# Attention and experts on one core: row scaling put behind the expert choices, row numbers as a sum of tensors, own rooms' gathers asked for sooner, gathered rows turned in three steps

## The chip, the cores and the metric

The kernel runs on one core of a Trainium2 chip. A core has TensorE (PE, matrix products), VectorE (DVE), ScalarE (ACT), GpSimd (POOL) and SyncE (SP), which starts plain transfers; POOL starts the indirect ones (gathers and scatters). The metric is the device time of one execution in microseconds. Each time comes from a median of runs, and one more execution was profiled.

## The reference

```python
# attention: 8 batches, 8 heads, 576 tokens, 64 per head, window of 128, a slope per head
scores = scale * q @ k.T - slope[h] * |rel|      # only 0 <= rel < 128
attn = softmax(scores);  x = (attn @ v) as rows of 512
# experts: per batch, a token takes its own best expert or that of the token before it
fresh_e = argmax(x[b, s] @ w_gate)
e = fresh_e if s == 0 or local_gate[b, s] < 0.5 else prev_e
out[b, s] = softmax(logits[b, s])[e] * (relu(x[b, s] @ w1[e]) @ w2[e])
```

## The kernel before, in words

**Attention.** 35 slots in a row work on 32 pairs of heads, four pairs for a batch. What each engine issues in a slot stands in a table of atoms (`ORDER`): scores `S`, minima `D`, exponentials `E`, transposes `U`, copies `C`, products `M`, results `X`, and `T`, in which DVE transposes the pair's result into the batch's tile `T`. The engines `pe`, `dve`, `act`, `pool` are wrapped in `InOrder`, so each runs its instructions in the order in which the program writes them. Between the atoms, "." advances `side`, the work of the batch that has just ended, and ":", ";" and "," advance three more generators, `gathers`, `early` and `turns`.

**The work of a batch** (`batch_side`) has two halves that advance by turns. `tokens` and `route` compute logits and choices: POOL copies the reciprocals into `rn`, PE makes the logits through the PSUM tile `pk` (its pool has one buffer), DVE forms the products `lw`, then `rm`, `ra`, `rc` and `rcb`, the choice in figures; PE and DVE spread them along the tokens (`hr`), give `OH`, and POOL scatters five times into the table `t4` (`t<-pay,to`). `scaled` is the other half: POOL makes 16 more copies into `rn` and multiplies the four parts of `T` by it (`T<-T,rn`); in the last batch DVE does this on `kr` (`kr<-kr,rn`). `store` then writes `T` to `xd` in DRAM, from which all gathers read.

**Rooms.** The expert part works through rooms, each for one expert. Three own rooms have a fixed expert and size: own0 (256 tokens), own1 (384) and own2 (256); the ranked rooms follow. Own0 and own1 take only tokens of the first batches as far as the tables of batches 5 and 6 know them, and their gathers can run before attention ends. `indices` turns a table into row numbers `xidx` (table entry plus `roff`). A gather (`gather`, POOL, L196) brings 32 rows of a quarter to SBUF; `split_x` turns four of them: DVE transposes into `xtr` (one buffer), ACT casts to `qx`'s high half, DVE subtracts for the low half. Each room has products `h` (with w1) and `y` (with w2), each as three products of halves; `hh` (ACT) and `hl` (DVE) are the halves of `h`, and weights come through `wraw` and are cut into halves `cut` by ACT and DVE.

**What paces the rooms.** `Fixed.run` calls `feed.tick` at points of its program. A tick advances `side` (the routing of batch 7, then the tables of the ranked rooms), turns one tile whose last gather was issued at least `LAG` ticks ago, and issues one gather. `feed.gather` issues none as long as batch 7 is not in `laid`; `ahead` holds gathers that were issued during attention. At a room's end `feed.finish` issues and turns what the next room still lacks.

## Time and profile before

| | |
|---|---|
| median of 3 runs | 691.26 us (690.39 to 691.51) |
| profiled execution | 690.55 us, span 688.8 us |
| mean granted TensorE clock | 0.981 |
| PE busy | 647.2 us, 94% of the span |
| DVE busy | 459.6 us, 67% |
| ACT busy | 413.8 us, 60% |
| POOL busy | 350.2 us, 51% |

The span runs from the first to the last instruction. The granted clock is a share of TensorE's full 2.4 GHz. Attention runs from 0 to about 236 us, own0 from 241.5, own1 from 277, and the ranked rooms from 342. An idle time of an engine stands in brackets in a timeline, with what ended it.

### The profile page before, as it was taken

What the parts mean: (1) busy time and instruction counts of PE and PEld (TensorE: products, weight loads), DVE (VectorE), ACT (ScalarE), POOL (GpSimd) and SP (SyncE); (2) the same over time, 40 slices, a digit from 0 to 9 for tenths busy, and PEclk for the clock granted to TensorE, in tenths of its full rate; (3) what the DMA queues carried; (4) which work ended last, traced back from release to release, by engine and by line L of the source; (5) the groups of instructions that cost most, each with busy time, mean ns of one, the idle gap of its engine ahead of it and who ended that gap; (6) DMA issues with size and microseconds to landing.
All of it is one profiled execution on the core that took longest, in us unless ns stands there. A gap on an engine that the chain in (4) does not pass through costs nothing. (4 is left out here: it accounts for less than half of the span.)

```text
span 688.8 us, 17129 instructions
## 1 busy us (share of the span) xinstructions
PE 647.2 (94%) x5929; PEld 533.8 (77%) x5929; DVE 459.6 (67%) x1434; ACT 413.8 (60%) x1229; POOL 350.2 (51%) x564
## 2 busy tenths in 40 slices
PE   8999999999998579999899999999999999999995
PEld 4777777777675367788689889888888888888884
DVE  7686877778778468776676477475637376655761
ACT  6889898898896553435455465354535354545541
POOL 6365474564737558424777476555735344321011
PEclk9999999999999978999999999999999999999998
DMA  7564765856585067646667577555847566665610
GB/s 233 188 234 138 250 218 153 299 167 211 193 291 168 13 201 234 224 129 209 199 203 242 160 230 239 175 175 173 307 146 273 179 206 224 195 240 167 250 35 31
DMA packets 50314, 134.41 MB, mean 195 GB/s; under 512 B 10967, under 2 KB 13655, under 8 KB 47922
## 3 DMA queue, kind: packets, MB, share of 16 engines
q1 hardware_dynamic: 40706, 113.43, 49.4%
q0 software_dynamic: 9088, 19.29, 9.7%
q8 instruction: 47, 0.77, 0.5%
q10 hardware_dynamic: 432, 0.59, 0.3%
q14 instruction: 41, 0.34, 0.2%
HBM read 113.67 MB, written 19.65 MB: 194 GB/s over the span
## 5 line engine op out<-in xcount | busy, mean ns | idle before, releaser
L196 POOL DMA_INDIRECT kr<-xd,xidx x141 | 160.5, 1138 | 46.1 <-issue 38.3
L291 DVE TENSOR_TENSOR cut<-wraw,cut 128x512 fp32r<-128x512 f32 x215 | 139.5, 685 | 43.2 <-ACT cut L289 41.5
L1008 PE MATMUL h<-qx,cut 128*128 128x256 f32 (+8 forms) x440 | 140.4, 319 | 1.2 <-ACT qx L205 1.2
L1009 PE MATMUL h<-qx,cut 128*128 128x256 f32 (+8 forms) x440 | 139.2, 317 | 0.3 <-DVE qx L206 0.3
L1010 PE MATMUL h<-qx,cut 128*128 128x256 f32 (+8 forms) x440 | 139.5, 317 | 0.0
L289 ACT CAST cut<-wraw 128x512 fp32r<-128x512 f32 x190 | 108.8, 617 | 37.1 <-PE y L1010 37.1
L993 POOL DMA_INDIRECT out<-y,sidx x41 | 45.4, 1107 | 166.2 <-ACT y L1020 133.8
L171 ACT ACTIVATE cut<-scs,mn 128x192 f32<-128x192 f32 (+2 forms) x288 | 123.7, 434 | 8.9 <-DVE mn L171 8.1
L1010 PE MATMUL y<-cut,hl 128*128 128x512 f32 (+2 forms) x288 | 113.0, 396 | 6.3 <-DVE hl L1114 6.2
L1008 PE MATMUL y<-cut,hh 128*128 128x512 f32 (+2 forms) x288 | 114.1, 396 | 2.0 <-ACT hh L171 1.9
L1009 PE MATMUL y<-cut,hh 128*128 128x512 f32 (+2 forms) x288 | 113.9, 395 | 0.0
L1113 ACT ACTIVATE hh<-h 128x256 fp32r<-128x256 f32 (+8 forms) x100 | 45.0, 450 | 114.4 <-PE h L1010 114.0
L1114 DVE SCALAR_TENSOR_TENSOR hl<-h,hh 128x256 fp32r<-128x256 f32 (+8 forms) x112 | 55.5, 495 | 75.8 <-ACT hh L1113 73.5
L171 DVE CUSTOM_DVE_ANT_0 scs<-sc,bias 128x192 f32<-128x192 f32 (+2 forms) x288 | 83.6, 323 | 29.7 <-PE sc L171 19.8
L1008 PEld LDWEIGHTS h<-qx,cut 128*128 128x128 f32 x440 | 84.0, 191 | 15.3 <-issue 9.1
L1009 PEld LDWEIGHTS h<-qx,cut 128*128 128x128 f32 x440 | 84.2, 191 | 4.3 <-DVE qx L206 0.5
L1010 PEld LDWEIGHTS h<-qx,cut 128*128 128x128 f32 x440 | 84.2, 191 | 0.3
L171 PE MATMUL sc<-kr,qx 64*64 64x192 f32 (+2 forms) x1280 | 72.0, 307 | 1.5 <-DVE mn L171 1.5
L1010 PEld LDWEIGHTS y<-cut,hl 128*128 128x128 f32 (+2 forms) x288 | 53.6, 187 | 21.1 <-DVE hl L1114 8.9
L171 PE MATMUL pt<-ident,cut 128*128 128x128 f32 x384 | 62.1, 286 | 0.6 <-DVE mn L171 0.6
L1008 PEld LDWEIGHTS y<-cut,hh 128*128 128x128 f32 (+2 forms) x288 | 54.0, 187 | 11.0 <-ACT hh L171 2.6
L1009 PEld LDWEIGHTS y<-cut,hh 128*128 128x128 f32 (+2 forms) x288 | 53.8, 187 | 9.0 <-issue 0.2
(195 smaller groups left out, 920.3 us busy)
## 6 DMA issues: line engine op xcount, KB each, us to landing
wraw<-w SPq DMA_DIRECT2D x112, 512.0 KB
xT<-w SPq DMA_DIRECT2D x10, 1024.0 KB
kr<-kT SPq DMA_DIRECT2D x31, 288.0 KB
qx<-qT SPq DMA_DIRECT2D x30, 288.0 KB
xd<-T SPq DMA_DIRECT2D x7, 1152.0 KB
v<-v SPq DMA_DIRECT2D x22, 256.0 KB
v<-v SPq DMA_DIRECT2D x32, 128.0 KB
cut<-v SPq DMA_DIRECT2D x10, 256.0 KB
```

What stands on the lines that cost most here:

```text
L171: ins = getattr(self.engine, name)(*args, **kw)
L196: queued(nc.gpsimd.indirect_dma_start(out=r, out_offset=None, in_=src[0:n, :], in_offset=bass.IndirectOffsetOnAxis(ap=col, axis=0), bounds ...
L289: scalar.copy(c[:, 0, f], raw[:, f])
L291: (pool if 2 * n + f == POOL_CUT else vector).tensor_tensor(c[:, 1, f], raw[:, f], c[:, 0, f], ALU.subtract)
L993: ins = nc.gpsimd.indirect_dma_start(out=out[:, :], out_offset=bass.IndirectOffsetOnAxis(ap=col[0:n], axis=0), in_=y[0:n], in_offset=None, ...
L1008: nc.tensor.matmul(o, ah, bh, start=start, stop=False)
L1009: nc.tensor.matmul(o, ah, bl, start=False, stop=False)
L1010: nc.tensor.matmul(o, al, bh, start=False, stop=stop)
L1113: now.act.activation(hh, hp, AF.Relu)
L1114: nc.vector.scalar_tensor_tensor(hl, hp, 0.0, hh, ALU.max, ALU.subtract)
```

## The change

- `scaled`: for all batches but the last, the four scalings of `T` are written only when `route` has appended the batch to `picked` (behind `rcb`), and behind the rooms 4 x `now.calm` further steps. `stores` now gets the batch when the copies are written; the store itself is written when the last scaling is (`scaled_rows`).
- `indices`: `xidx` is a `tensor_tensor` sum with `roff` broadcast instead of a `tensor_scalar` with a value per partition.
- `gathers` is advanced at atom `E5` too, and run to its end behind the last slot; `feed.gather` now holds back as long as batch 7 is in `stores`.
- `split_x` yields between its three steps; `Feed` does one step a tick, `flush` finishes a tile that has been begun. `LAG` is 14 instead of 10.
- `now.held` marks where a tile `pk` is waiting for its reader, and `early` waits while it is set.

```diff
--- before.py
+++ after.py
@@ -182,7 +182,7 @@
         return ins
 
     class Now:
-        calm = 0
+        calm, held = 0, False
 
     now = Now()
 
@@ -202,12 +202,14 @@
         pin(nc.vector.transpose(t, r.rearrange("p q c -> p (q c)")))
         v = t.rearrange("p (q c i) -> p c q i", q=n, c=4)
         xh, xl = (x.rearrange("p c (q i) -> p c q i", q=n) for x in (xh, xl))
+        yield
         now.act.copy(xh, v)
+        yield
         nc.vector.tensor_tensor(xl, v, xh, ALU.subtract)
 
     t4v = t4.rearrange("(t k) w -> t k w", t=32)
 
-    entered, latest, laid, ahead, written = [], [], [], [], []
+    entered, latest, laid, ahead, written, picked, scaled_rows, stores = [], [], [], [], [], [], [], []
 
     def load_table(c0, n, block):
         ins = nc.sync.dma_start(xs[:, c0:c0 + n], t4v[:, block:block + n] if isinstance(block, int) else t4v[:, bass.ds(block, n)])
@@ -223,7 +225,7 @@
 
     def indices(vector, c0, n, w0, wins):
 
-        vector.tensor_scalar(xidx[:, c0:c0 + n], xt[:, c0:c0 + n, 0], roff[:, 0:1], None, ALU.add)
+        vector.tensor_tensor(xidx[:, c0:c0 + n], xt[:, c0:c0 + n, 0], roff.broadcast_to([P, n]), ALU.add)
         yield
         m = len(wins)
         f = tp.tile([P, 48, 2, 4], F32, name="fw", bufs=1)[:, :m]
@@ -264,13 +266,13 @@
                 self.xh, self.xl = self.x[:, 0], self.x[:, 1]
             n = self.last(t)
             sl = slice(P * t, P * t + 32 * n)
-            split_x(self.r[:, t, :n], self.xh[:, :, sl], self.xl[:, :, sl], n)
+            return split_x(self.r[:, t, :n], self.xh[:, :, sl], self.xl[:, :, sl], n)
 
     def at_once(r):
         for t in range(r.n):
             for q in range(4):
                 r.take(t, q)
-            r.turn(t)
+            run(r.turn(t))
 
     def load_chunk(e, which, c):
         src = w1 if which == "a" else w2
@@ -631,16 +633,19 @@
             yield
             for lo, n in ((0, 512), (512, 64)):
                 yield from calm()
+                now.held = True
                 pk = ptk.tile([P, 512], F32, name="pk")
                 for k in range(4):
                     pe.matmul(pk[32 * k:32 * k + 32, :n], w32[:, k], xT[:, k, lo:lo + n], start=True, stop=True)
                 yield
                 act.copy(part[:, lo:lo + n], pk[:, :n])
+                now.held = False
                 yield
             read.append(b)
             by_head = rn[:, 72:112].rearrange("p (h x) -> p x h", h=2)
             for t0, n in ((0, 4), (4, 1)):
                 yield from calm()
+                now.held = True
                 pk = ptk.tile([P, n, 4, 32], F32, name="pk")
                 for t in range(n):
                     pe.transpose(pk[:, t], part[:, P * (t0 + t):P * (t0 + t) + P], ident)
@@ -648,6 +653,7 @@
                 w = tp.tile([P, 16, 2, 9], F32, name="lw", bufs=1)[:, :4 * n]
                 dve.tensor_tensor(w, pk.rearrange("p t k (h f) -> p (t k) h f", h=2)[:, :, :, 0:9],
                                   by_head[:, 4 * t0:4 * t0 + 4 * n].unsqueeze(3).broadcast_to([P, 4 * n, 2, 9]), ALU.mult)
+                now.held = False
                 dve.tensor_reduce(L[:, t0:t0 + n], w.rearrange("p (t k) h e -> p t e (k h)", k=4), AX.X, ALU.add)
                 yield
 
@@ -668,14 +674,17 @@
                             q = 64 * g + 32 * a
                             pool.tensor_copy(rows[q:q + 32, :, o::2, z], rb[c:c + 32, :, o:9:2])
                     yield
+            stores.append(b)
             laid.append(b)
-            while ("T1", 4 * b + 3) not in emitted:
+            while ("T1", 4 * b + 3) not in emitted or b < NB - 1 and b not in picked:
+                yield
+            for _ in range(4 * now.calm):
                 yield
             for p in range(4):
                 t = T[b][:, :, p]
                 (pool if b < NB - 1 else dve).tensor_tensor(t, t, RN[b % 2][:, 18 * p:18 * p + 18].unsqueeze(2).broadcast_to([P, SB, 32]), ALU.mult)
                 if p == 3:
-                    stores.append(b)
+                    scaled_rows.append(b)
                 yield
             if b == NB - 1:
                 store(b)
@@ -704,10 +713,12 @@
             dve.tensor_tensor(a5, a5, k8, ALU.mult)
             dve.tensor_reduce(c, a5, AX.X, ALU.max)
             dve.tensor_tensor(cb, c, fr, ALU.mult)
+            picked.append(b)
             yield
             hr = HR[b % 2]
             for lo, n in ((0, 512), (512, 64)):
                 yield from calm()
+                now.held = True
                 pr = ptk.tile([1, 512], F32, name="pk")
                 w = min(P, n)
                 for t in range(lo // P, (lo + n + P - 1) // P):
@@ -718,8 +729,10 @@
                 yield
                 dve.tensor_tensor_scan(hr[:, lo:lo + n], hold[:, :n], pr[:, :n],
                                        0.0 if lo == 0 else hr[:, lo - 1:lo], ALU.mult, ALU.add)
+                now.held = False
                 yield
             yield from calm()
+            now.held = True
             ph = ptk.tile([P, NT, NE], F32, name="pk")
             for t in range(NT):
                 pe.matmul(ph[:, t], hr[:, P * t:P * t + P], onesb[0:1, 0:NE], start=True, stop=True)
@@ -730,11 +743,13 @@
             yield
             act.activation(ex, ex, AF.Exp)
             dve.tensor_tensor(OH, ph, k8, ALU.is_equal)
+            now.held = False
             yield
 
             assert all(i in bumped for i, n in enumerate(EARLY) if n <= b)
             yield from calm()
             aid = pool if b < NB - 1 else dve
+            now.held = True
             pr = ptk.tile([P, NT, NE], F32, name="pk")
             pe.matmul(pr, utri, OH, start=True, stop=False)
             for t in range(1, NT):
@@ -751,6 +766,7 @@
             rk = tp.tile([P, NT, NE], F32, name="rk")
             ri = tp.tile([P, NT], I32, name="ri")
             dve.tensor_tensor(rk, pr, OH, ALU.mult)
+            now.held = False
             pool.tensor_tensor(pay[:, b, :, 2], gt, se, ALU.mult)
             with nc.allow_low_precision("small whole numbers"):
                 dve.tensor_reduce(ri, rk, AX.X, ALU.add)
@@ -781,6 +797,8 @@
         def early(group):
             while EARLY[group[0]] - 1 not in routed:
                 yield
+            while now.held:
+                yield
             pn = ptk.tile([P, NE], F32, name="pk")
             pe.matmul(pn, onesb, ohs, start=True, stop=True)
             for i in group:
@@ -791,7 +809,9 @@
                 dve.tensor_tensor(ohs[0:1, e:e + 1], ohs[0:1, e:e + 1], d[0:1], ALU.add)
                 bumped.append(i)
                 load_table(col_of[i], OWN_BLOCKS[i], BPE * e)
-            for _ in range(8):
+            for _ in range(5):
+                yield
+            while now.held:
                 yield
             copies(pe, act, col_of[group[0]], sum(OWN_BLOCKS[i] for i in group))
             yield
@@ -828,7 +848,7 @@
                     yield
                 for _ in range(6):
                     yield
-                r.turn(t)
+                yield from r.turn(t)
                 yield
             while not W.raw or NB - 2 not in read:
                 yield
@@ -838,7 +858,7 @@
                     yield
                 yield from W.split(W.room(), act, dve)
 
-        known, bumped, taken, routed, read, emitted, inverted, stores = [], [], [], [], [], [], [], []
+        known, bumped, taken, routed, read, emitted, inverted = [], [], [], [], [], [], []
         rows0 = [Rows(col_of[i], win_of[i], OWN[i][1], n) for i, n in enumerate(EARLY)]
         side, prep = iter(()), {":": setup(), ";": iter(())}
         pairs = {}
@@ -852,7 +872,7 @@
                 else:
                     if i % 11 == 0:
                         yield from ";,"
-                    yield from {"E8": ":", "E3": ":"}.get(atom.strip("'"), "")
+                    yield from {"E8": ":", "E3": ":", "E5": ":"}.get(atom.strip("'"), "")
 
         for slot in range(4 * NB + DEPTH):
             b, p = divmod(slot, 4)
@@ -894,11 +914,11 @@
                     side = batch_side(n // 4, pairs[n][1].xT)
             if 1 <= slot < 4 * NB - 1:
                 values(slot + 1)
-            for n in list(stores):
+            for n in [n for n in stores if n in scaled_rows]:
                 store(n)
             if p == 1 and b + 1 < NB:
                 loaded = load(b + 1)
-        run(chain(prep[";"], prep[","], side))
+        run(chain(prep[";"], prep[":"], prep[","], side))
         last_xT = xT
 
 
@@ -1150,7 +1170,7 @@
         def turn(self, t):
             x = tp.tile([P, 2, 4, P], F32R, name="xT")
             self.xh, self.xl = x[:, 0], x[:, 1]
-            split_x(self.row, self.xh, self.xl)
+            return split_x(self.row, self.xh, self.xl)
 
         def run(self, W, tick):
             y = py.tile([P, DM], F32, name="y")
@@ -1224,10 +1244,10 @@
         table_done.append(1)
 
     class Feed:
-        LAG = 10
+        LAG = 14
 
         def __init__(self, side):
-            self.side, self.clock, self.at, self.turns, self.items = side, 0, 0, [], []
+            self.side, self.clock, self.at, self.turns, self.items, self.step = side, 0, 0, [], [], iter(())
             fixed = [i for i, v in enumerate(visits) if isinstance(v, Fixed)] + [len(visits)]
             for i in [x for a, b in zip(fixed, fixed[1:]) for x in [b] + list(range(a + 1, b)) if x < len(visits)]:
                 r = visits[i].rows
@@ -1245,7 +1265,7 @@
         def gather(self, upto):
             if self.at == len(self.items):
                 return False
-            if NB - 1 not in laid:
+            if NB - 1 in stores or NB - 1 not in laid:
                 return False
             while self.items[self.at] in ahead:
                 ahead.remove(self.items[self.at])
@@ -1266,9 +1286,14 @@
             for x in self.turns:
                 if x[0] <= upto and self.clock >= x[2] + lag:
                     self.turns.remove(x)
-                    visits[x[0]].rows.turn(x[1])
+                    self.step = visits[x[0]].rows.turn(x[1])
+                    next(self.step)
                     return True
             return False
+
+        def flush(self):
+            run(self.step)
+            self.step = iter(())
 
         def tick(self, upto, turn=True):
 
@@ -1276,7 +1301,7 @@
             next(self.side, None)
             if route_done:
                 now.act = nc.scalar
-            if turn:
+            if next(self.step, 0) == 0 and turn:
                 self.turn(upto, self.LAG)
             self.gather(upto)
             if pending and self.clock % 3 == 0:
@@ -1287,9 +1312,11 @@
                 while not self.known(self.items[self.at][0]):
                     next(self.side, None)
                 if not self.gather(upto):
+                    self.flush()
                     assert self.turn(upto, 0)
+            self.flush()
             while self.turn(upto, 0):
-                pass
+                self.flush()
 
     feed = Feed(routing())
     now.act = act
```

Where the order of instructions moves, place by place:

POOL in batch 6, at the end of attention, before the change (`rn` are the copies, `T` the scaling, `wraw<-xd` the gathers of own0):

```order
L171 COPY rn_95<-rb_93 32x4x4 x4
L171 TENSOR_TENSOR T_160<-T_160,rn_95 128x18x32
L196 DMA wraw<-xd,xidx 128x128
L171 TENSOR_TENSOR T_160<-T_160,rn_95 128x18x32 x3
L196 DMA wraw<-xd,xidx 128x128 x3
L171 TENSOR_TENSOR rch<-rex,OH 128x40
```

and with the change:

```order
L171 COPY rn_95<-rb_93 32x4x4 x4
L196 DMA wraw<-xd,xidx 128x128 x3
L171 TENSOR_TENSOR T_160<-T_160,rn_95 128x18x32 x3
L196 DMA wraw<-xd,xidx 128x128
L171 TENSOR_TENSOR T_160<-T_160,rn_95 128x18x32
L196 DMA wraw<-xd,xidx 128x128
L171 TENSOR_TENSOR rch<-rex,OH 128x40
```

Three gathers now stand ahead of the scaling, and all of own0's are out before the choice's last part (`rch`).

POOL from batch 6's last choice to batch 7's copies (`t` is the table `t4`, `kr<-xd` are the gathers of own1), before:

```order
L171 TENSOR_TENSOR ohs<-ohs,cn 128x8
L770 DMA t_76<-pay,to 40960x4 x2
L196 DMA wraw<-xd,xidx 128x128
L770 DMA t_76<-pay,to 40960x4 x3
L196 DMA wraw<-xd,xidx 128x128
L196 DMA kr<-xd,xidx 128x128 x4
L171 COPY rn_96<-rb_94 64x4x5 x4
```

and with the change:

```order
L171 TENSOR_TENSOR ohs<-ohs,cn 128x8
L196 DMA kr<-xd,xidx 128x128
L786 DMA t_76<-pay,to 40960x4 x2
L196 DMA kr<-xd,xidx 128x128
L786 DMA t_76<-pay,to 40960x4 x3
L196 DMA kr<-xd,xidx 128x128 x10
L171 COPY rn_96<-rb_94 64x4x5 x4
```

Ahead of the copies stood 11 indirect transfers, and now stand 17, all twelve gathers of own1 among them.

DVE in own0, before, where it turns tiles of own1 (`xtr`, `qx`) between the halves of own0's `h` (`hl`):

```order
L171 TENSOR_TENSOR ra<-lg_98,rm 128x40
L202 STREAM_TRANSPOSE xtr<-kr 128x512
L171 TENSOR_TENSOR ra<-ra,k_82 128x40
L171 TENSOR_REDUCE rc<-ra 128x5
L171 TENSOR_TENSOR rcb<-rc,rf 128x5
L206 TENSOR_TENSOR qx<-xtr,qx 128x4x128
L1114 SCALAR_TENSOR_TENSOR hl<-h,hh 128x256
L291 TENSOR_TENSOR cut<-wraw,cut 128x512 x2
L202 STREAM_TRANSPOSE xtr<-kr 128x512
L206 TENSOR_TENSOR qx<-xtr,qx 128x4x128
```

and with the change, at the end of own0 (128x256 is own0's `hl`, the last one; `y` is its result):

```order
L1134 SCALAR_TENSOR_TENSOR hl<-h,hh 128x256
L293 TENSOR_TENSOR cut<-wraw,cut 128x512 x2
L171 SCALAR_TENSOR_TENSOR hr_105<-hold,hr_105,pk 1x64
L202 STREAM_TRANSPOSE xtr<-kr 128x512
L293 TENSOR_TENSOR cut<-wraw,cut 128x512 x2
L1038 TENSOR_SCALAR y<-y,sg 128x512
L208 TENSOR_TENSOR qx<-xtr,qx 128x4x128
L171 TENSOR_TENSOR rex<-lg_98,rm 128x40
L202 STREAM_TRANSPOSE xtr<-kr 128x512
L171 TENSOR_TENSOR OH<-pk,k_82 128x40
L208 TENSOR_TENSOR qx<-xtr,qx 128x4x128
L202 STREAM_TRANSPOSE xtr<-kr 128x512
```

The three turns of own1, which stood between own0's steps, now stand behind its last `hl`; the third ends after the rows shown.

## Rows read from the trace of the kernel before

**Rows 1.** Timeline of PE, 205 to 300 us: start, duration, instruction, [idle before, releaser].
```profile
218.96 0.39 PE L171 MATMUL pk<-identb,rcb 128*1 128x128 f16 x4 [2.84 <-DVE rcb L171]
241.50 0.80 PE L1008 MATMUL h<-qx,xT 128*128 128x256 f32 x2 [5.91 <-ACT qx L205]
258.20 0.79 PE L1010 MATMUL y<-cut,hl 128*128 128x512 f32 x1 [3.69 <-DVE hl L1114]
276.96 0.33 PE L1008 MATMUL h<-qx,cut 128*128 128x384 f32 x1
287.92 0.50 PE L1008 MATMUL y<-cut,hh 128*128 128x512 f32 x1 [1.09 <-ACT hh L171]
```

**Rows 2.** Timeline of PE, 325 to 347 us.
```profile
331.34 0.50 PE L1010 MATMUL y<-cut,hl 128*128 128x512 f32 x1 [1.83 <-DVE hl L1114]
342.28 0.50 PE L1008 MATMUL h<-qx,cut 128*128 128x256 f32 x2 [1.23 <-ACT qx L205]
```

**Rows 3.** Windows: us, busy PE, PEld, DVE, ACT, POOL, PEclk, DMA, GB/s.
```profile
219.00:223.00 4.00, 4.00 (x49) 2.98 (x51) 3.83 (x17) 2.27 (x7) 1.23 (x2) 0.57 0.56 185
256.50:263.50 7.00, 5.30 (x19) 4.72 (x20) 6.97 (x13) 0.00 (x0) 5.78 (x5) 0.52 0.79 269
```

**Rows 4.** Timeline of DVE, 210 to 222 us.
```profile
213.29 3.44 DVE L171 TENSOR_SCALAR xidx<-xt,roff 128x12 int32<-128x12 f32 x1
...
218.27 0.20 DVE L171 TENSOR_TENSOR ra<-ra,k 128x40 f32<-128x40 f32 x1
```

**Rows 5.** Timeline of POOL, 204 to 226 us.
```profile
206.03 4.77 POOL L171 COPY rn<-rb 64x20 f32<-64x20 f32 x19 [1.66 <-DMA t<-pay,to]
...
213.31 3.38 POOL L171 TENSOR_TENSOR T<-T,rn 128x576 f32<-128x576 f32 x3
```

**Rows 6.** Timeline of DVE, 226 to 262 us.
```profile
240.08 0.71 DVE L202 STREAM_TRANSPOSE xtr<-wraw 128x512 f32<-128x512 f32 x1 [5.18 <-DMA wraw<-xd,xidx]
...
254.46 1.43 DVE L171 TENSOR_TENSOR kr<-kr,rn 128x576 f32<-128x576 f32 x2 [4.67 <-POOL rn L171]
```

**Rows 7.** Timeline of POOL, 226 to 260 us.
```profile
238.69 1.02 POOL L196 DMA_INDIRECT kr<-xd,xidx  x1 [0.31 <-issue]
240.01 1.00 POOL L196 DMA_INDIRECT kr<-xd,xidx  x1 [0.30 <-issue]
...
243.15 1.50 POOL L196 DMA_INDIRECT kr<-xd,xidx  x1 [0.30 <-issue]
...
249.66 4.76 POOL L171 COPY rn<-rb 64x20 f32<-64x20 f32 x19 [2.29 <-DMA kr<-xd,xidx]
```

**Rows 8.** Timeline of DVE and POOL, 46 to 48.7 us.
```profile
44.95 3.42 POOL L171 TENSOR_TENSOR T<-T,rn 128x576 f32<-128x576 f32 x3
...
47.39 1.03 DVE L171 TENSOR_TENSOR ra<-ra,k 128x40 f32<-128x40 f32 x1
```

**Rows 9.** Transfers of `xd`, 195 to 262 us, from issue to landing.
```profile
DMA to landing us min/median/max: 2.6/3.8/6.3
```

**Rows 10.** Timeline of PE, 246 to 259 us.
```profile
247.37 0.40 PE L1008 MATMUL y<-cut,hh 128*128 128x512 f32 x1
...
248.75 0.28 PE L1008 MATMUL h<-qx,cut 128*128 128x256 f32 x1
```

**Rows 11.** Timeline of ACT, 268 to 292 us.
```profile
272.61 0.62 ACT L171 CAST qx<-xtr 128x512 fp32r<-128x512 f32 x1 [1.65 <-DVE xtr L202]
...
277.97 1.14 ACT L171 CAST cut<-wraw 128x512 fp32r<-128x512 f32 x2 [1.54 <-PE y L1010]
279.01 0.68 ACT L171 ACTIVATE y<-y,sg 128x512 f32<-128x512 f32 x1
```

**Rows 12.** Timeline of DVE, 268 to 292 us.
```profile
273.26 0.69 DVE L206 TENSOR_TENSOR qx<-xtr,qx 128x512 fp32r<-128x512 f32 x1 [0.69 <-ACT qx L171]
```

**Rows 13.** Timeline of DVE, 325 to 346 us.
```profile
330.13 0.71 DVE L202 STREAM_TRANSPOSE xtr<-kr 128x512 f32<-128x512 f32 x1 [4.16 <-DMA kr<-xd,xidx]
```

**Rows 14.** Timeline of ACT, 325 to 346 us.
```profile
344.32 0.62 ACT L205 CAST qx<-xtr 128x512 fp32r<-128x512 f32 x1 [1.57 <-DVE xtr L202]
```

## Prediction

> **What bounds the kernel now.** TensorE (PE) is busy 94% of the span, so I read first where it stops. The timeline of PE, with what ended each stop, has four stops that the change can touch before the ranked rooms: 2.84 us in batch 6 for the choices `rcb`, 5.91 us ahead of own0's first `h` for the turned rows, 3.69 us inside own0 for `hl`, and 1.09 us in own1 [rows 1]. A fifth stands where own2 becomes the first ranked room: 1.83 us and then 1.23 us [rows 2]. Each of the longer stops is paid twice. In 219 to 223 us, behind the 2.84 us stop, the mean granted clock is 0.57 with PE busy all the time, and in 256.5 to 263.5 us, around the 3.69 us stop, it is 0.52 [rows 3]: TensorE is then at its lower level, 1.2 GHz. That is 0.43 x 4.0 = 1.7 us lost behind the one, and 0.48 x 5.3 busy us, about 2.5, behind the other.
>
> Behind the stops stand these. At 213.29 the row numbers `xidx` take VectorE (DVE) 3.44 us [rows 4], exactly as long as GpSimd (POOL) scales three parts of `T` [rows 5]; the choices queue behind. At 240.08 DVE has waited 5.18 us for the last gather of own0 [rows 6]. In own0 DVE waits 4.67 us for POOL's 20 `rn` copies, ahead of `hl` in its order [rows 6]; these copies wait until the gathers issued before them have landed (the last one runs 243.15 to 244.65, the copies resume at 249.66) [rows 7]. This last wait decides my forecast.
>
> **The change part by part.** *Scaling behind the choices.* POOL's order in batches 1 to 4 is the same as before, and each scaling waits only for the copies, the earlier store and DVE's transposes. So the mid-batch stops stay, and I count 0. On SP the store of `T` moves behind one set of `v` loads, and in batch 6 the `xs` loads ahead of one set; `T` has two buffers, so the store delays no one, and the `v` loads cost PE 0 to 1 us, of which I take 0. `held` only keeps `early` from taking the one `pk` buffer between a product and its reader: 0. In batch 6 the order does change: three gathers now stand ahead of the scaling (first place shown above). The copies that ran at 206.03 for 4.77 us [rows 5] come 1.3 later, since one gather more stands ahead of them, and end at 212.1; three gathers on it is 216.2, and four scalings of 1.15 with a gather between end at 222.2. All eight gathers of own0 are out at 223; before, the last came just ahead of 238.69 [rows 7].
>
> *Row numbers as a sum of tensors.* With gathers beside it, a two-input operation of DVE is not held: `ra<-ra,k` takes 0.20 us at 218.27 [rows 4], and 1.03 us at 47.39, where it ends with POOL's third scaling [rows 8]. The 12-column sum at 213.3 meets gathers, so the 2.84 us stop and its 1.7 us of clock go: 4.5 us. Given back are about 3.1: the 8-column sum and the `fw` products now meet the scaling at 216 to 222 (two waits of up to 1.03), and the first turn's subtraction stands ahead of `OH` on DVE and waits for ScalarE's cast (about 1.0). The attention part ends 1.4 us earlier; own0's rows are turned by then, so own0 starts at 235.6 - 1.4 = 234.2 instead of 241.50: 7.3 us, and at the upper clock, another 2.5.
>
> The Trainium skill (SBUF — State Buffer, § Who interferes with whom) says that a DVE instruction with two SBUF inputs contends with a GpSimd instruction that reads SBUF, and that the one that issues first holds the shared pair for its whole instruction. By that rule the sum is held wherever it meets a scaling, so it is no cure in itself; the trace agrees with it in the 1.03 us at 47.39. By the rule the end of attention gains the 1.4 us, without it some 3.4.
>
> *Gathers sooner, in own0.* POOL now issues 12 gathers of own1 and batch 6's five scatters, 17 in all, before the `rn` copies of batch 7 (second place shown); before, it issued 11. The first of them needs batch 6's store, which starts with the end of the scaling; the longest landing in this stretch is 6.3 us [rows 9], so it goes at 228.5. From start to start a gather here takes (243.15 - 238.69)/3 = 1.49 us, beside 1.00 + 0.30 = 1.30 at best [rows 7]; I take 1.42. Then 228.5 + 16 x 1.42 + 1.1 = 252.3. Behind the last, the copies waited 1.66 us in batch 6 after scatters [rows 5] and 5.0 us in own0, where weights were loading [rows 7]; I take 2.2, nearer to the first, since PE will have stopped and frees no weight buffers. So the copies run at 254.5 to 259.3 (4.76 us [rows 7]); before they ended at 254.42.
>
> Who waits: the second group of logit transposes needs the one `pk` buffer, which DVE frees only with the first four copies. By the order some 13 us of work stand between own0's first `h` and that group, so PE reaches it at about 247 and stands until 255.9, some 8.5 us, where it stood 3.69 before. Then DVE has three `kr<-kr,rn` of 0.72 ahead of `hl` [rows 6]: 259.3 + 2.15 + 0.42 = 261.9. What is left of own0 there: before, from 258.20 to 276.96 it took 18.76 us [rows 1], less 2.6 of clock, and less two `y` and two `h` that are done already, 1.4 each (six matmuls of `y` run from 247.37 to 248.75 [rows 10]; twelve of `h` have as many columns), 5.7. So 10.4 us, and own0 ends at 272.3.
>
> *LAG 14 and three steps, own0 to own1.* Before, three of own1's tiles were turned during own0 (third place shown). Now all three stand at its end, behind the last `y`, one after the other because `xtr` has one buffer: ScalarE's two casts 1.14 and `y` 0.68 [rows 11]; cast 0.62, subtract 0.69, transpose 0.71 [rows 6, 11, 12] with two small operations (0.3), cast 0.62, subtract and transpose 1.40, cast 0.62. Together 6.8 us of idle PE, and own1 starts at 279.1 instead of 276.96. Of own0, 0.46 us was still done behind that start before, so +1.7. The idle 6.8 us then costs the clock, 2.5 as behind the 3.69 us stop [rows 3]: +2.5. Own1's own 1.09 us stop, for a gather's turn in its midst [rows 1], goes: -1.1.
>
> *Own2 to the first ranked room.* DVE's 4.16 us in the middle of own2 [rows 13] goes, since that turn is no longer there, and PE's 1.83 us with its clock (1.7, as behind the 2.84): -3.5. Both turns now stand at the end; `h` starts when the second cast is done, which in the times of before is 344.32 + 0.62 = 344.94 [rows 14], where it started at 342.28 [rows 2]: +2.7. A stop of 1.23 + 2.7 = 3.9 us is as long as one that cost the clock: +1.8, near the lower of the two prices.
>
> In the later rooms PE has no stops to lose or gain, and the three steps only change places on DVE and ScalarE: 0. **Sum:** +1.7 + 2.5 - 1.1 - 3.5 + 2.7 + 1.8 = +4.0. The gain of 9.8 us at own0's start is inside the first term; the copies and the boundary eat it. The profiled execution took 690.55 (its span of 688.8 and what lies around it), which gives 694.55; the median of the runs lies 0.7 above that execution, so a median of after may lie a little above, too. I forecast **694.6 us**.
>
> **Bounds of the unknown.** The chain of 17: at 1.30 each and landing in 1.66, own0 ends 2.5 us sooner (692.1); at 1.49 and 5.0, 4 us later (698.6). The clock behind the two boundaries: 0 at least and 5.0 at most in all, so down to 690. The likeliest case's own range is 691.5 to 698.6.
>
> **Rivals.** *PE stands only shortly in own0 (faster).* If the copies do not wait for the gathers' landing or PE need not stand for them, own0 keeps its start of 234.2 and runs as before with one stop of 3.69 us: from 241.50 to 276.96 it took 35.5, less 2.5 of clock and the 0.46 behind it, so it ends at 266.7; the boundary adds 6.8, and own1 starts at 273.5. That is 3.9 us sooner by the reckoning that gave +1.7, so the time is 694.6 - 5.6 = 689.0. It decides from the point where PE stands under 4 us in own0. Against it: the copies waited for indirect transfers in [rows 5] and in [rows 7]. If the boundary is shorter too (turns dropped in between), 686. Chance 0.25.
>
> *Same.* The short end of the chain (692.1) and one boundary without loss of clock (-2.1) give 690 to 692.6. Chance 0.15.
>
> *The copies late (slower still).* POOL's gathers land at 5.0 us because the weights load during them, as at 243.15: 698.6, and with a later store 700. For it: own0's weights are asked for in that stretch too. Chance 0.15, beside 0.45 for the forecast itself.
>
> *The sum does not free the choices.* If POOL comes late enough to scale at 213 to 216, DVE's sum is held there by the scaling, 1.03 us as in [rows 8] instead of 3.44, and the choices come about 1 us later than I say. POOL's store sets the next stretch and not the choices, so the end moves by less than 1 us, to 695.5 at most. Chance 0.1, inside the forecast's own share. The rule of the Trainium skill named above (SBUF — State Buffer, § Who interferes with whom) would then hold at this place.
>
> **How the numbers follow.** Faster or slower means by over 0.2% (1.4 us), about what a measurement of this kernel can tell from no change: below 689.9, or above 692.6. Slower 0.60 (forecast and late copies), same 0.15, faster 0.25. The range reaches into the faster rival and to the late copies: 688 to 699.5, with 0.1 outside at either end.
>
> **What would show it.** PE idle about 8 us near 247 to 256, released through `lw` and POOL's `rn`, and DVE's wait for `rn` near 259; own0's first `h` near 234; an idle PE of 6 to 7 us ahead of own1's first `h`, ended by a cast, and a clock near 0.5 behind it; about 4 us ahead of the first ranked room; no `xidx` of 3.4 us at 213. I am wrong if the copies start before 250, or if own1's turns run before own0 ends.

## The result and the profile after

| | before | after |
|---|---|---|
| median | 691.3 us (690.13 to 692.47) | 695.48 us (694.06 to 699.18) |
| profiled execution, span | 690.55, 688.8 | 699.18, 697.5 |
| mean granted clock | 0.981 | 0.972 |
| PE, DVE, ACT, POOL busy | 647.2, 459.6, 413.8, 350.2 | 651.6, 462.9, 414.9, 347.9 |

The ratio is 1.0069, 95% interval 1.0043 to 1.0096, from six runs of each, taken together: slower by 4.2 us, where 3.3 (694.6) was forecast. The profiled execution of after is the longest of its six, 3.7 us above their median. It can be taken apart at the first `h` of own0, own1 and the first ranked room (the start of each in the timeline of PE; forecasts from the prediction's working; before and after sum to their spans):

| stretch, us | before | forecast | after |
|---|---|---|---|
| start to own0 | 241.50 | 234.2 | 240.89 |
| own0 to own1 | 35.46 | 44.9 | 44.47 |
| own1 to first ranked room | 65.32 | 65.5 | 63.82 |
| from there to the end | 346.5 | 348.3 | 348.3 |

The second stretch and the last came as forecast. The first ends 6.7 us late, and the third is 1.7 us shorter than forecast. Together that is 4.6 us over the forecast in this execution, which itself lies 3.7 above the median. The timeline of PE answers to [rows 1] and [rows 2] (lines in kernel.py moved by 20):

```profile
191.92 0.59 PE L171 MATMUL pk<-identb,rcb 128*1 128x128 f16 x4 [2.20 <-DVE rcb L171]
...
222.89 0.39 PE L171 MATMUL pk<-identb,rcb 128*1 128x128 f16 x4 [0.32 <-DVE rcb L171]
...
231.54 0.18 PE L171 MATMUL pk<-OH,utri 128*128 128x40 f16 x1 [1.46 <-DVE OH L171]
...
240.89 0.39 PE L1028 MATMUL h<-qx,xT 128*128 128x256 f32 x1
...
262.10 0.47 PE L171 MATMUL pk<-ident,part 128*128 128x128 f32 x1 [7.59 <-DVE lw L171]
...
282.67 0.19 PE L171 MATMUL pk<-OH,utri 128*128 128x40 f16 x1 [3.65 <-DVE OH L171]
285.36 1.01 PE L1028 MATMUL h<-qx,cut 128*128 128x384 f32 x2 [2.36 <-ACT qx L171]
...
349.18 0.80 PE L1028 MATMUL h<-qx,cut 128*128 128x256 f32 x2 [3.92 <-ACT qx L206]
```

Batch 6's stop of 2.84 us for `rcb` is 0.32, and own0's first `h` waits for nothing. The stops of 7.59, of 3.65 and 2.36 ahead of own1, and of 3.92 ahead of the first ranked room are those forecast. Grown is the first line: 2.20 us for the choices of batch 5, where PE stood 0.91 before. The list of PE's waits from 0 to 205 us (us in total, times, longest) shows that it is not alone. Its row before and then after:

```profile
PE pk L171 <- DVE rcb L171: 4.2, 6, 0.9
```

```profile
PE pk L171 <- DVE rcb L171: 7.1, 6, 2.2
```

Around that stop stand these, on POOL and on DVE:

```profile
184.50 3.38 POOL L171 TENSOR_TENSOR T<-T,rn 128x576 f32<-128x576 f32 x3
188.18 1.10 POOL L196 DMA_INDIRECT wraw<-xd,xidx  x1 [0.30 <-DVE mn L171]
189.30 1.17 POOL L171 TENSOR_TENSOR T<-T,rn 128x576 f32<-128x576 f32 x1
```

```profile
186.90 1.00 DVE L171 TENSOR_TENSOR xidx<-xt,roff 128x8 int32<-128x8 f32 x1
...
188.56 2.02 DVE L171 TENSOR_TENSOR fw<-xt,msel 128x8 f32<-128x8 f32 x2
...
191.70 0.17 DVE L171 TENSOR_TENSOR rcb<-rc,rf 128x5 f16<-128x5 f32 x1
```

`xidx` ends with POOL's third scaling, at 187.9, and the `fw` products with its fourth, at 190.5. Before, this batch's four scalings stood ahead of most of the choice and ended at 186.75:

```profile
182.26 4.49 POOL L171 TENSOR_TENSOR T<-T,rn 128x576 f32<-128x576 f32 x4
```

The windows of after (as in [rows 3]: us, busy PE, PEld, DVE, ACT, POOL, PEclk, DMA, GB/s) show what stops cost in clock:

```profile
191.10:197.90 6.80, 5.98 (x59) 4.59 (x60) 5.05 (x23) 3.15 (x12) 0.58 (x1) 0.52 0.70 205
...
279.80:290.10 10.30, 5.07 (x21) 4.73 (x21) 5.62 (x11) 2.29 (x5) 7.09 (x7) 0.52 0.70 240
348.10:354.90 6.80, 5.72 (x25) 5.50 (x26) 1.49 (x3) 1.00 (x2) 5.00 (x6) 0.52 0.54 169
```

Behind batch 5's stop 0.48 x 5.98 = 2.9 us are lost. That may be most of the 3.7 by which this execution lies above the median; the other five executions have no profile to show it. At batch 6 and in own0, POOL's timeline answers to [rows 5] and [rows 7]:

```profile
212.90 4.75 POOL L171 COPY rn<-rb 64x20 f32<-64x20 f32 x19 [1.60 <-DMA t<-pay,to]
217.92 1.07 POOL L196 DMA_INDIRECT wraw<-xd,xidx  x1 [0.27 <-POOL rn L171]
219.29 1.00 POOL L196 DMA_INDIRECT wraw<-xd,xidx  x1 [0.30 <-issue]
220.60 1.00 POOL L196 DMA_INDIRECT wraw<-xd,xidx  x1 [0.30 <-issue]
221.66 3.39 POOL L171 TENSOR_TENSOR T<-T,rn 128x576 f32<-128x576 f32 x3
...
234.64 1.08 POOL L196 DMA_INDIRECT kr<-xd,xidx  x1 [0.69 <-PE pt L171]
...
257.31 1.00 POOL L196 DMA_INDIRECT kr<-xd,xidx  x1 [0.30 <-issue]
258.31 0.23 POOL L171 COPY rn<-rb 64x20 f32<-64x20 f32 x1
260.81 4.74 POOL L171 COPY rn<-rb 64x20 f32<-64x20 f32 x19 [2.28 <-DMA kr<-xd,xidx]
```

And DVE's answers to [rows 4] and [rows 6]:

```profile
219.74 0.17 DVE L171 TENSOR_TENSOR xidx<-xt,roff 128x12 int32<-128x12 f32 x1
...
221.92 0.92 DVE L171 TENSOR_TENSOR rcb<-rc,rf 128x5 f16<-128x5 f32 x1
...
224.65 0.43 DVE L171 TENSOR_TENSOR xidx<-xt,roff 128x8 int32<-128x8 f32 x1
...
226.59 0.95 DVE L171 TENSOR_TENSOR fw<-xt,msel 128x8 f32<-128x8 f32 x2
...
261.59 0.46 DVE L171 TENSOR_TENSOR lw<-pk,rn 128x288 f32<-128x288 f32 x1 [8.06 <-POOL rn L171]
...
265.58 2.10 DVE L171 TENSOR_TENSOR kr<-kr,rn 128x576 f32<-128x576 f32 x3 [2.82 <-POOL rn L171]
```

In batch 6 three gathers stand beside `xidx` of 12 columns, which takes 0.17 us; of the choice only `rcb` meets a scaling, the first (0.92). The `xidx` and `fw` of 8 columns, which come later, meet the others (0.43 and 0.95). From 234.64 to 258.31 POOL issues 17 gathers and scatters, 1.42 us apart on average ((257.31 - 234.64)/16), then the copies wait 2.28 us for the last gather to land.

### The profile page after: what moved, and what is told of

It reads as the page before. It is cut to its first block, busy times and chain, and to the rows that moved or that the text cites. A ratio compares the mean times of both kernels' runs of the same rounds, so it can differ in the third digit from the quotient of the medians.

```text
span 697.5 us, 17122 instructions
## 1 busy us (share of the span) xinstructions
PE 651.6 (93%) x5929; PEld 538.5 (77%) x5929; DVE 462.9 (66%) x1434; ACT 414.9 (59%) x1229; POOL 347.9 (50%) x564
## 5 line engine op out<-in xcount | busy, mean ns | idle before, releaser
L196 POOL DMA_INDIRECT kr<-xd,xidx x141 | 158.0, 1121 | 54.2 <-issue 39.6
L1028 PEld LDWEIGHTS h<-qx,cut 128*128 128x128 f32 x440 | 85.1, 194 | 20.6 <-issue 9.5
L1029 PEld LDWEIGHTS h<-qx,cut 128*128 128x128 f32 x440 | 85.2, 194 | 4.2 <-DVE qx L208 0.4
L1030 PEld LDWEIGHTS h<-qx,cut 128*128 128x128 f32 x440 | 85.2, 194 | 0.1
```

Source lines behind the costliest of these rows:

```text
L196: queued(nc.gpsimd.indirect_dma_start(out=r, out_offset=None, in_=src[0:n, :], in_offset=bass.IndirectOffsetOnAxis(ap=col, axis=0), bounds ...
L1028: nc.tensor.matmul(o, ah, bh, start=start, stop=False)
L1029: nc.tensor.matmul(o, ah, bl, start=False, stop=False)
L1030: nc.tensor.matmul(o, al, bh, start=False, stop=stop)
```

## The experiments

Two theories stood against each other. The rooms: 12 gathers of own1 ahead of the `rn` copies, with the later turns, cost more than the new order in attention earns (A, where an expectation uses letters). Against it, attention: DVE's two-input operations are still held by POOL's scaling, which "behind the choices" only writes later and does not make wait. Every ratio is against the kernel before in the same set of runs.

**After again, and two parts of it.** In this set of runs the kernel before itself took 753.56 us. e1 is after unchanged; e2 and e3 are:

```diff
 # e2: own1's gathers not ahead of the copies
-            while 1 not in known or ("S8", 4 * NB - 1) not in emitted:
...
-                    ahead.append((1, t, q))
-                    yield
-            if NB - 1 in stores or NB - 1 not in laid:
+            if NB - 1 not in laid:
 # e3
-        LAG = 14
+        LAG = 10
```

> The changed kernel as it is, once more, with a profile of its own. Theory A (the rooms: copies of batch 7 behind own1's twelve gathers, own1's turns at own0's end, both followed by the lower clock): 695 us (694 to 697), PE stops 7 to 9 us in own0 until DVE's lw, about 6 us ahead of own1 and 3.9 us ahead of the first ranked room, while attention up to batch 6's logits takes as long as before, within 2 us. Rival B (attention: the sum and the fw products are held by the scaling in batch 5, and rcb in batches 0 and 1): again a stop of about 2.2 us ahead of batch 5's choices with the lower clock behind it, and attention 4 us or more longer than before; the rooms then explain at most 2 us.

> The changed kernel, but own1's gathers are left to the rooms' ticks, which issue them as before as soon as batch 7's copies are written: POOL then has only the five scatters ahead of the copies. Theory A: the stop of 7.6 us in own0 falls below 1 us, own1's first h comes some 8 to 12 us sooner, counted from own0's first h, and the time is 687 us (685 to 690). Rival B: the rooms give nothing, because own1 then waits for its later gathers: 694 to 696.

> The changed kernel with LAG 10. Its order has one of own1's transposes ahead of own0's last hl and the turn in the middle of own2 again. Theory A: the stop ahead of own1 falls from 6 to about 4.5 us, that ahead of the first ranked room from 3.9 to about 1.3, and 1.8 us with its clock come back in own2: 694 us (692.5 to 695.5). Rival (LAG is what costs): 691 to 692.

e1 took 773.74 us (1.0232, 1.016 to 1.0304), e2 763.05 (1.0148, 1.0099 to 1.0198), e3 775.02 (1.0316, 1.0248 to 1.0384). e1's list of waits has rows of PE without a recorded releaser, such as this one:

```profile
PE y L1028 <- issue: 14.3, 3, 5.5
```

With these, terms of a few us can't be read in this set, so the three expectations can be neither met nor refuted by it. What holds: after is slower here too, every run of e2 is faster than every run of e1, and LAG 10 alone gives nothing back that can be seen.

**The sum alone**, in that set (e4) and in another (e10), as an edit of the kernel before:

```diff
-        vector.tensor_scalar(xidx[:, c0:c0 + n], xt[:, c0:c0 + n, 0], roff[:, 0:1], None, ALU.add)
+        vector.tensor_tensor(xidx[:, c0:c0 + n], xt[:, c0:c0 + n, 0], roff.broadcast_to([P, n]), ALU.add)
```

> The kernel before with the row numbers as a sum of tensors and nothing else. Theory A: the sum at batch 6 takes 1.0 to 1.2 us beside the scaling instead of 3.44, so the stop ahead of the choices falls from 2.84 to about 0.6 us, but own0 still waits for its last gather behind the scatters, so the end moves by 1 to 3 us: 689 us (688 to 691). Rival (the sum is held by all three scalings as the old form was): 691.3, within 0.7.

> The kernel before with the sum of tensors alone, once more, since the first run of it stood beside a kernel before of 753 us. Theory A: at batch 6 the sum ends with one scaling, 1.0 to 1.2 us instead of 3.44, the stop for the choices falls from 2.84 to below 1 us, but own0 waits for its last gather behind the scatters all the same: 689.5 us (688 to 691). Rival (no effect): 691.2, within 0.7, with the sum held for 3 us.

e4: 752.59 us (0.9991, 0.9955 to 1.0028). e10: 692.07 (688.0 to 694.12) beside 690.84, ratio 1.0013 (0.999 to 1.0035). The timelines of DVE and POOL in e10, batch 6:

```profile
214.03 0.17 DVE L171 TENSOR_TENSOR xidx<-xt,roff 128x12 int32<-128x12 f32 x1
...
214.85 3.54 DVE L171 TENSOR_TENSOR fw<-xt,msel 128x12 f32<-128x12 f32 x2
```

```profile
214.90 3.38 POOL L171 TENSOR_TENSOR T<-T,rn 128x576 f32<-128x576 f32 x3
```

`xidx` is free because a gather stands beside it; the pair `fw` behind it is held just as long. PE waits 2.88 us for `rcb`, as in [rows 1]. By itself the sum earns nothing: e10 went with its rival, no effect, though not with the reason that the rival gave, since `xidx` was free. e4's interval is too wide to tell.

**Copies first again (e5)**, the edit of e2 in a set where the kernel before took 691.15 us.

> The same kernel as in the run that leaves own1's gathers to the rooms' ticks, because the kernel before itself took 753 us there, 9% over its other runs, and PE stood for up to 7 us at a time where the profile shows no releaser; that hides terms of a few us. If the kernel before takes about 691 us here, theory A expects 687 us (685 to 690), own0's stop for lw below 1 us and own1's first hl some 8 us sooner after own0's first hl than with the change; rival B (attention is what costs) 693 to 696.

691.53 us (687.31 to 696.1), 1.0002 (0.9979 to 1.0024). The stop for `lw` is gone, but 4.77 us for batch 7's `rcb` take its place; the timelines of POOL, of DVE and of PE:

```profile
240.82 8.73 POOL L171 COPY rn<-rb 64x20 f32<-64x20 f32 x20 [4.21 <-DVE rb L171]
```

```profile
260.07 0.71 DVE L202 STREAM_TRANSPOSE xtr<-kr 128x512 f32<-128x512 f32 x1 [4.51 <-DMA kr<-xd,xidx]
260.71 0.15 DVE L171 TENSOR_REDUCE rc<-ra 128x5 f32<-128x40 f32 x1
```

```profile
261.12 0.59 PE L171 MATMUL pk<-identb,rcb 128*1 128x128 f16 x4 [4.77 <-DVE rcb L171]
```

The turn of own1's first tile, whose gather now comes late, stands ahead of `rc` and `rcb` in DVE's order. So the transfers ahead of the copies are a cause of the loss (e5 is level with the kernel before, 1.0002, where after has 1.0069), but to take all 12 gathers away is no cure: 687 was expected and missed by 4.5 us.

**The scaling really waits (e6)**: after, and POOL's first scaling of batches 0 to 6 waits for `rcb`.

```diff
+                if p == 0 and b < NB - 1:
+                    tc.add_manual_dep(ins.ins, choice[b], mybir.DependencyInfo(mybir.DependencyClass.Sync, mybir.DependencyReason.DATA), reason="choice")
...
-            dve.tensor_tensor(cb, c, fr, ALU.mult)
+            choice[b] = dve.tensor_tensor(cb, c, fr, ALU.mult).ins.name
```

> The changed kernel with one wait added: in batches 0 to 6 POOL's first scaling of T waits for rcb, so that the scaling really runs behind the choices. Theory A (the waits of the choices in the middle of a batch come from two-input operations of DVE that meet the scaling): PE's stops for rcb, some 7 us in all in either kernel, fall below 2 us, and the time falls by 3 to 6 us against the changed kernel, to about 691. Rival (the scaling then meets hr, OH and the fw products, or batch 6's store comes later and with it the gathers of own1 and the copies): the stops for OH grow by as much, or own0's stop grows by 2 us, and the time stays within 1.5 us of the changed kernel.

688.85 us (686.21 to 689.86), 0.9959 (0.9942 to 0.9975): 6.6 below after's median, which comes from another set. POOL and DVE in batch 5, and then PE's waits from 205 to 290 us:

```profile
184.09 3.38 POOL L171 TENSOR_TENSOR T<-T,rn 128x576 f32<-128x576 f32 x3 [5.32 <-issue]
```

```profile
182.44 0.23 DVE L171 TENSOR_TENSOR fw<-xt,msel 128x8 f32<-128x8 f32 x2
...
183.78 0.17 DVE L171 TENSOR_TENSOR rcb<-rc,rf 128x5 f16<-128x5 f32 x1
```

```profile
PE pk L171 <- DVE lw L171: 8.0, 1, 8.0
PE pk L171 <- DVE OH L171: 5.3, 2, 3.7
PE h L1031 <- ACT qx L171: 2.4, 1, 2.4
```

POOL, whose row names no releaser, stands 5.32 us and starts 0.14 us behind `rcb`'s end; `fw` takes 0.23 us instead of 2.02. Up to 205 us PE's list has no row for `rcb`. Batch 6's `rcb` comes at 212.20, 9.7 us sooner than in after's profiled execution; the rooms keep their stops. So attention holds a part of the loss and the rooms, by e5, another.

**The rooms undone (e7)**, and with the wait of e6 (e8): after with own1's first four gathers ahead instead of 12, the old gate, LAG 10 and turns in one step.

```diff
-            for t in range(r.n):
+            for t in range(1):
...
-            if NB - 1 in stores or NB - 1 not in laid:
+            if NB - 1 not in laid:
...
-        LAG = 14
+        LAG = 10
...
-                yield from r.turn(t)
+                run(r.turn(t))
```

> The changed kernel with its part in the rooms undone: four of own1's gathers ahead of batch 7's copies instead of twelve, the tick's gate and LAG 10 as before, tiles turned in one step. The attention part stays as changed. Theory A: own0's stop falls from 7.6 to 3 us or less, own1 is turned during own0, so own1's first hl comes 36 to 39 us after own0's (45.2 with the change, 36.2 before), and the stop ahead of the first ranked room is about 1.3 us again; with own0 starting some 6 us sooner than before the time is 685 us (683 to 689). Rival (gathers sooner is no gain, since attention's choices wait longer): 690 or more.

> The same with the scaling made to wait for rcb in batches 0 to 6. Theory A, both parts: attention 6 us shorter by batch 6's choices and no stop for rcb over 0.5 us, the rooms as in the run with four gathers ahead; 680 us (678 to 683). Rival (the store of batch 6 comes later behind the held scaling, so that the rooms give the gain back, as they did with twelve gathers ahead): 686 to 690.

e7: 689.77 us (688.33 to 690.68), 0.9985 (0.9971 to 0.9999), 5.7 below after. e8: 684.59 (683.04 to 686.07), 0.9914 (0.9892 to 0.9936), 5.2 below e7 in the same set. Both sizes were missed by 4.6 to 4.8 us, and both lie between the ranges of theory and rival. In their rooms PE stands elsewhere now; e7's waits from 205 to 290 us, where before stood 1.9 us for `hh`:

```profile
PE y L1028 <- ACT hh L171: 10.2, 5, 4.1
```

**The best (e9)**: e8 with LAG 14 and turns in three steps kept; that is e6 with only four gathers ahead and the old gate.

> The same, but with LAG 14 and the three steps of the change kept, so that these two alone differ. Theory A: own1's and the first ranked room's turns stand later, a stop of 3.9 us and the lower clock come back ahead of the first ranked room, where 1.8 us in own2 go: 1 to 4 us slower than the run with one step and LAG 10, 683 us (680 to 686). Rival (the steps pay for themselves because DVE no longer waits for ScalarE's cast): the same within 1 us or faster.

683.69 us (682.05 to 684.56), 0.9902 (0.988 to 0.9923): 5.2 below e6 by the medians, 3.9 by the ratios of the two sets, and no slower than e8, where 1 to 4 us slower was expected. Of e9, PE's waits from 205 to 290 us:

```profile
PE y L1031 <- ACT hh L171: 7.5, 3, 4.5
PE pk L171 <- DVE OH L171: 3.2, 2, 2.8
```

and behind 290 us:

```profile
PE h L1031 <- ACT qx L206: 3.9, 1, 3.9
```

No wait for `lw` is in the list, but 7.5 us for `hh` are. From own0's first `h` to that of the first ranked room e9 takes 103.7 us, e7 103.9 and e8 104.1, where after takes 108.3 and e6 108.8: so with four gathers ahead the rooms are some 5 us shorter in the traces too. Before, that way took 100.8; e9's gain on it lies ahead of own0, which starts at 231.63 instead of 241.50. The three steps and LAG cost nothing in sum that can be told, though the 3.9 us ahead of the first ranked room are theirs: e8's longest there is 1.2. e9 beats both kernels, the one before by 1%.

**Which parts are needed (e11, e12)**, in a set where the kernel before took 743.39 us: e11 is the kernel before with the scaling written behind `rcb` and waiting for it; e12 has that and the sum, with rooms and gathers as before (it keeps `held` and the later store of after).

```diff
 # e11, beside e6's lines
-            while ("T1", 4 * b + 3) not in emitted:
+            while ("T1", 4 * b + 3) not in emitted or b < NB - 1 and b not in choice:
```

> The kernel before with one thing changed: POOL's first scaling of T waits for rcb in batches 0 to 6. Theory A (the held scaling ends the stops for the choices, and the rooms follow, since they wait for chains that start at batch 6's choices): batch 6's rcb 5 to 7 us sooner, the stop of 2.84 us gone, own0 still waiting 4 to 6 us for its last gather; 685.5 us (683.5 to 687.5). Rival (own0 waits for its gathers until about the same time as before, because the held scaling and store push them back, so that the gain of attention is lost without gathers sooner): 689 to 691.

> The same with the sum of tensors as well, own0's gathers at the places of before and the rooms as before. Theory A: the sum adds nothing once the scaling waits; the same as the wait alone within 1 us. Rival (the old form of the row numbers still costs 1 us or more beside the scaling or a gather): 1 to 2 us faster than the wait alone.

e11: 744.7 us (1.0018, 0.9978 to 1.0059); e12: 746.99 (1.0035, 1.0004 to 1.0067). The 685.5 expected of e11 was not tested fairly: neither list has a large wait for `rcb` up to 205 us, but the stops without a releaser are there again, and in such a set little may be left to win (e4, without the wait, stands only 0.7 us for `rcb` up to there). Whether the wait alone would give the 5 us where the kernel before takes 691 stays open. Nor can e12 tell whether the sum adds anything then.

## Why the prediction came close, and where it was wrong

The median lies 0.9 us above the forecast, partly by luck: attention came out later than worked out, own1 to the ranked rooms shorter. (The rounded terms of its sum add up to 4.1; unrounded they give the 4.0.)

**The rooms were right.** The 17 transfers, the copies behind their landing, PE's stop (7.59 us; forecast 8.5), the turns at own0's end (3.65 + 2.36 = 6.0; 6.8) and ahead of the first ranked room (3.92; 3.9) came as worked out: from own0 to own1 44.47 us for 44.9. The clock behind own0's end cost 0.48 x 5.07 = 2.4 (2.5 forecast), that behind the last boundary 0.48 x 5.72 = 2.7, not 1.8; that the ranked rooms still agree to the tenth is in part luck. e9 shows the cause by taking it away: with four gathers ahead, e6's 8.0 us for `lw` are gone. The gate of before is back in the same kernel, so the shares of gate and gathers are not told apart.

**The wrong step is "so the mid-batch stops stay, and I count 0".** It looked at batches 1 to 4 and left out 0 and 5. In the profiled execution batch 6's first product `lw` comes 6.46 us later than before (218.39 for 211.93): 2.9 from stops for `rcb` (7.1 less 4.2), 2.9 from the clock behind batch 5's, 0.7 not traced. Of the 2.9 in stops, 1.3 are batch 5's (2.20 for 0.91), 0.8 batch 0's and 0.9 batch 1's (1.79 for 0.87); batch 2's fell by 0.1. POOL's order in batch 1 is that of before by the prediction's reading, and the stop there is 1.53 in e10, which has the old order too, and 1.02 in e7, so it varies with more than that order. Batch 5's stop is there in e5 (1.93) and e7 (2.17) too, without a fall of the clock; so the clock's 2.9 seem to belong to this execution, and without them its 699.18 would be near 696.3. Batch 0's stop went from 0.69 to 1.45, with two copies of `v` now ahead of the scaling on POOL. e6 shows the cause: with the scaling behind the choice in time and not only in writing, these stops are gone.

**"Two waits of up to 1.03" held at its own place, but not as a price.** In batch 6, for which it was written, the `xidx` and `fw` of 8 columns took 0.43 and 0.95 us, within the bound. Taken as the most that one meeting costs it is too low: the pair `fw` took 3.54 us in e10, over three scalings on end, and 2.02 in batch 5 of after, over the rest of a gather and the scaling behind it. The Trainium skill (SBUF — State Buffer, § Who interferes with whom) says that a DVE instruction with two SBUF inputs contends with a GpSimd instruction that reads SBUF, and that the one that issues first holds the shared pair for its whole instruction. The runs agree that they contend; by one instruction the price would be at most 1.17, the time of one scaling, and the 3.54 measured is three times that. Who is held does not follow the rule in these two rows: by the profile `fw` starts ahead of the scaling in both (214.85 for 214.90, 188.56 for 189.30), and yet DVE is the one that stands. A gather was still running on POOL in both when `fw` started; what part it had no run shows.

**The sum earned nothing by itself.** The prediction booked 4.5 us at batch 6 under it. The stop went, but because three gathers stand where three scalings stood, which the prediction saw too; e10, with the sum and the old order, keeps 2.88. Whether the new order needs the sum no run shows. The rival "the sum does not free the choices" did not come at batch 6, but its mechanism is what happened in batch 5, where a scaling holds `xidx` for 1.00 us.

**Own1 to the ranked rooms** took 1.7 us less than forecast. Products through `pk` are 0.6 of it: they took 1.85 us there before and 1.25 after, since batch 7's routing gets further inside own0. The other 1.1 us is not traced.

**The rivals.** "PE stands only shortly" and "the copies late" did not come: the copies resumed 2.5 us behind the end of the last gather (260.81 for 258.31), 2.2 was taken. "Same" did not come either. Seen from batch 6's logits, own0 started at 240.89 - 6.46 = 234.4 and own1 at 278.9, where the prediction said 234.2 and 279.1.

## What to carry to other kernels

Work that is written later in an engine's program need not run later in time: in batch 5 of after POOL scaled while DVE still chose. Where two engines hold each other, make the one wait for the other's result, if its own has slack: here a wait of 5.3 us on POOL earned 5 to 7 us on the path. Count what an in-order engine issues ahead of a computation that waits for landings: twelve gathers put ahead instead of four, with the gate that goes with them, cost 4 to 5 us. An execution that agrees with a sum in total still has to be compared stretch by stretch, since two terms of 2 to 4 us can hide each other.

## What the runs showed of the hardware

- DVE was held over three scalings of POOL in a row: 3.54 us beside 3.38, for the pair `fw` of 12 columns in e10, which took 0.25 when free in batch 6 of e6.
- A stop of about 2 us sometimes costs the clock and sometimes not: 0.52 behind 2.20 us in after's profiled execution, 1.00 behind 2.17 in e7 and 1.93 in e5.
- POOL's 20 `rn` copies took 8.73 us in e5, where DVE cut weights at the same time, and 4.97 in after, where DVE stood.
- On two sets of runs the kernel before took 753.6 and 743.4 us, 8 to 9% more than elsewhere, with stops of PE (up to 5.5 us in e1, 7.6 in e4) that no recorded event ends. Their cause stays open. The record gives the set with 743.4 the same chip number (12) as that of e5 and e6 with 691.15, so the number of the chip does not explain it.
